# Sparse attention with a four-expert layer on one core: both phase-1 experts loaded early, probabilities normed before the split, q and k turned by DMA

## The chip, the cores and the metric

One core of one Trainium2 chip runs the kernel. The metric is device time in microseconds (us); a lower time is better. TensorE (PE) multiplies, VectorE (DVE), ScalarE (ACT) and GpSimd (POOL) do elementwise work, and SyncE (SP) only issues DMAs. Each engine runs its own instructions in the order in which the program lists them.

## The reference

```python
def _attn_ref(q, k, v, tau):                 # q, k, v: (4, 8, 576, 64) float32
    scores = (1 / sqrt(64)) * q @ k.transpose(0, 1, 3, 2)
    thresh = max(scores, -1) - tau           # keep what is within tau of the row's largest
    scores = where(scores >= thresh, scores, -1e9)
    attn = exp(scores - max(scores, -1))
    attn = attn / (sum(attn, -1) + 1e-9)
    return attn @ v
# x: (2304, 512), the 4 * 576 tokens with their 8 heads side by side
def _moe_ref(x, domain_probs, w1, w2):       # w1: (4, 512, 1024), w2: (4, 1024, 512)
    p = domain_probs / (sum(domain_probs, -1) + 1e-9)
    return sum over e of p[:, e:e+1] * (maximum(x @ w1[e], 0) @ w2[e])
```

Every token goes through all four experts.

## The kernel before

**Numbers.** Where float32 accuracy is wanted at float16 speed, a value is scaled by a power of two and split into a high and a low float16 half, `hi = f16(s*a)` and `lo = f16(s*a - hi)`, and a product is three matmuls: hi·hi, hi·lo, lo·hi. ACT writes the high half, DVE or POOL the low one. Weights, V, q and k of batches 1 to 3, and the probabilities of these batches go this way. Batch 0 is done in plain float32.

**Attention.** The work is cut into 80 items: 4 batches, 4 pairs of heads, and 5 blocks of query rows (`j` = 0 to 3 with 128 rows for each head of the pair, `j` = 4 with the last 64). Item 20 is the first of batch 1. In an item PE makes the scores in the one PSUM tile S (`emit_qk`), DVE copies them to SBUF as SS and takes the row's extreme (`cm`, L931), POOL adds tau to it (tile sm, L946), ACT takes the exponential into E (L954), and DVE sets to zero what is below the threshold and sums the rows (L963, both inputs in SBUF). The probabilities then have to be turned for the product with V. In batch 0 PE turns E through PSUM (tile ET) and ACT copies it to PT. From batch 1 on E is split (ACT L1069, DVE L1073) and a DMA transpose brings both halves to PT (`spread`, `turn`). `group` multiplies with V (tile av), and norms last: reciprocals of the row sums are spread over partitions by small matmuls (tile rp, L1140 and L1148) and multiplied in. The result is split into X, the input of the experts.

q and k come to SBUF as raw; `t_prep` turns them on PE through the tile S (10 float32 transposes a pair of heads, L601 to L606), and from batch 1 on ACT and DVE split them out of PSUM into T.

**Experts.** `unit` takes a block of tokens through one expert: G1 (tile mm from X and W, L1284), ReLU and split into h on ACT and POOL (L1296, L1304, L1313), G2 (L1328), and the accumulation. Experts 0 and 1 are phase 1 and run between the items; their partial sums go to DRAM. Experts 2 and 3 are phase 2 and run when phase 1 is done, since the 16 weight tiles W hold two experts. `ready` hands a block to `unit` when all four pairs of heads are done for its rows. `passes` says which `j` make a block: in batch 0 (0), (1), (2, 3, 4), else (0, 1), (2, 3, 4). The last blocks of all, 256 and 128 tokens, can run only after the last item.

**Order.** The class `Plan` lists operations with a cost and a priority each (item number for attention, 1000 and more for the experts), and writes them out engine by engine in the order of its own schedule. Pools limit it: 3 tiles raw, 3 tiles ss (SS and the split E), 2 tiles PT.

## Time and profile before

| | before |
|---|---|
| median of 3 runs | 1057.08 us (1055.54 to 1059.47) |
| the profiled execution's own time | 1056.98 us |
| its span, first to last instruction | 1055.2 us |
| PE busy | 1011.8 us, 96% of the span |
| DVE, ACT, POOL busy | 568.9, 571.8, 238.8 us |
| G1 and G2 on PE (L1284, L1328), busy | 376.4 and 395.4 us |

The span is shorter than the time by what lies around the first and last instruction, 1.8 us. Busy time of PE counts overlapping matmuls once. A share of busy time is a mean over stages: attention with the experts between it, the rest of phase 1, and phase 2.

### The profile page before, as it was taken

How to read it: one execution, taken by the hardware profiler on the slowest of the kernel's cores; microseconds unless marked ns; L12 is line 12 of the kernel's file. 1: busy time of each engine (PE TensorE's matmuls, PEld its weight loads, DVE VectorE, ACT ScalarE, POOL GpSimd, SP SyncE). 2: the span in 40 equal slices, each digit the busy share in tenths (PEclk: the TensorE clock that was granted, in tenths of full speed). 3: DMA queues.
4: the chain of work that ended last, by engine and by line, in shares of the span. 5: the costliest groups of instructions: out<-in, count | busy, mean ns of one | idle time of the engine just before them, and what ended most of it. 6: DMA issues, size and time to landing. Idle time of an engine off the chain costs nothing.

```text
span 1055.2 us, 20513 instructions
## 1 busy us (share of the span) xinstructions
PE 1011.8 (96%) x7946; PEld 665.4 (63%) x7946; DVE 568.9 (54%) x1338; ACT 571.8 (54%) x1183; POOL 238.8 (23%) x399
## 2 busy tenths in 40 slices
PE   6679969999999999999999999998999999999997
PEld 4466746666666567665656676665766676677665
DVE  3786767988779887888874005563221222122222
ACT  4777767766676668765664355543432343234322
POOL 1113325433344335333332232100000000000000
PEclk9889978999999999999999999999999999999999
DMA  6900325656558667555665103420201101011000
GB/s 172 248 12 18 93 82 137 125 91 142 103 107 190 91 121 117 112 103 110 123 113 108 40 2 123 147 71 30 91 10 51 40 21 61 21 41 40 1 31 21
DMA packets 211970, 88.67 MB, mean 84 GB/s; under 512 B 178336, under 2 KB 198816, under 8 KB 211872
## 3 DMA queue, kind: packets, MB, share of 16 engines
q1 hardware_dynamic: 211872, 87.36, 36.4%
q8 instruction: 62, 1.02, 0.4%
q14 instruction: 36, 0.29, 0.1%
HBM read 40.93 MB, written 14.16 MB: 52 GB/s over the span
## 4 chain that ended last, share of the span: by engine, by line
PE 83%; DMA 5%; DVE 4%; SPq 3%; ACT 2%; issue 2%; POOL 1%; DVEq 0%; ACTq 0%; POOLq 0%
PE mm L1284 34%; PE mm L1328 33%; PE av L1174 4%; PE S L865 4%; SPq L380 3%; DMA PT<-E 3%; DMA wraw<-in_moe_w_dram 2%; PE S L876 1%; DVE E L963 1%; PE av L1183 1%; PE ET L983 1%; DVE SS L931 1%; PE S L601 1%; PE rp L1140 1%; PE S L870 1%
## 5 line engine op out<-in xcount | busy, mean ns | idle before, releaser
L1328 PE MATMUL mm<-W,h 128*128 128x512 f16 x1728 | 395.4, 379 | 0.0
L1284 PE MATMUL mm<-X,W 128*128 128x256 f16 (+1 forms) x3360 | 376.4, 270 | 3.0 <-ACT hr L1296 3.0
L1284 PEld LDWEIGHTS <-W 128*128 128x128 f16 x3744 | 343.2, 98 | 56.3 <-issue 3.2
L1296 ACT ACTIVATE hr<-mm,wc 128x256 f32<-128x256 f32 (+1 forms) x312 | 141.6, 456 | 283.0 <-PE mm L1284 279.0
L1328 PEld LDWEIGHTS <-h 128*128 128x128 f16 x1728 | 165.2, 98 | 175.5 <-issue 0.4
L1313 POOL TENSOR_TENSOR h<-hr,h 128x256 f16<-128x256 f32 (+1 forms) x168 | 115.9, 696 | 143.8 <-ACT h L1304 119.1
L963 DVE SCALAR_TENSOR_TENSOR E<-SS,sm,E 128x576 f32<-128x576 f32 x144 | 123.0, 865 | 17.1 <-ACT E L954 10.6
L1353 DVE SCALAR_TENSOR_TENSOR acc<-mm,psc,acc 128x512 f32<-128x512 f32 x54 | 38.9, 748 | 169.7 <-PE mm L1328 169.4
L1313 DVE TENSOR_TENSOR h<-hr,h 128x256 f16<-128x256 f32 x144 | 60.9, 425 | 125.5 <-ACT h L1304 125.3
L946 POOL TENSOR_SCALAR sm<-sm,tau_p 128x1 f32<-128x1 f32 x144 | 77.4, 538 | 215.8 <-DVE SS L931 160.0
L1304 ACT ACTIVATE h<-hr 128x256 f16<-128x256 f32 (+1 forms) x312 | 122.4, 397 | 6.4
L954 ACT ACTIVATE E<-SS,sm 128x576 f32<-128x576 f32 x144 | 108.4, 767 | 15.8 <-DVE SS L931 15.7
L1268 POOL TENSOR_SCALAR psc<-pnv,wpm 128x2 f32<-128x2 f32 (+1 forms) x39 | 18.3, 474 | 348.3 <-DVE acc L1353 268.1
L931 DVE TENSOR_SCALAR_CACHE_REDUCE SS<-S,qc 128x576 f32<-128x576 f32 x108 | 85.7, 813 | 18.6 <-PE S L876 8.5
L1069 ACT ACTIVATE E<-E 128x1152 f16<-128x1152 f32 (+1 forms) x72 | 65.4, 924 | 44.9 <-DVE E L963 23.7
L1073 DVE SCALAR_TENSOR_TENSOR E<-E,E 128x1152 f16<-128x1152 f32 (+1 forms) x72 | 76.6, 1078 | 11.8 <-ACT E L1069 11.8
L1174 PE MATMUL av<-PT,V 128*64 128x320 f16 (+3 forms) x768 | 62.5, 311 | 2.1 <-DMA PT<-E 2.1
L865 PE MATMUL S<-T 64*128 64x512 f16 (+1 forms) x352 | 59.9, 442 | 1.6 <-DVE SS L931 0.9
L809 DVE SCALAR_TENSOR_TENSOR W<-wraw,wsc,W 128x1024 f16<-128x1024 f32 x28 | 35.4, 1285 | 37.7 <-ACT W L784 37.6
L784 ACT ACTIVATE W<-wraw,wsc 128x1024 f16<-128x1024 f32 x32 | 35.3, 1143 | 24.7 <-DVE wsc L454 24.3
L931 DVE TENSOR_SCALAR_CACHE_REDUCE SS<-S,qs 128x576 f32<-128x576 f32 x36 | 28.7, 812 | 22.9 <-PE S L876 15.1
L1174 PEld LDWEIGHTS <-V 128*64 128x64 f16 x576 | 31.3, 109 | 10.9 <-issue 6.9
(114 smaller groups left out, 689.8 us busy)
## 6 DMA issues: line engine op xcount, KB each, us to landing
wraw<-in_moe_w_dram SPq DMA_DIRECT2D x64, 256.0 KB, 3.9
part<-acc SPq DMA_DIRECT2D x18, 256.0 KB, 2.2
X<-x_dram SPq DMA_DIRECT2D x9, 512.0 KB, 3.6
acc<-part SPq DMA_DIRECT2D x18, 256.0 KB, 2.8
raw<-in_q_dram SPq DMA_DIRECT2D x32, 128.0 KB, 3.0
raw<-in_k_dram SPq DMA_DIRECT2D x32, 128.0 KB, 3.2
out_dram<-acc SPq DMA_DIRECT2D x16, 256.0 KB, 2.3
x_dram<-X SPq DMA_DIRECT2D x7, 512.0 KB, 3.0
```

The costliest lines, as they stand in the source:

```text
L865: nc.tensor.matmul(ps[:, 1024 * h:1024 * h + SM], t[r, a, 128 * j:128 * j + 128], t[r, c, 704:1216], start=(y == 0), stop=(y == last),)
L931: nc.vector.tensor_scalar(out=pl.t(*ssu)[:, S * h:S * h + S], in0=pl.t(*su)[:, 960 * h:960 * h + S], scalar1=qc[:, g, 2:3] if g >= NP * T3 ...
L946: lambda h=h: nc.gpsimd.tensor_scalar(out=pl.t(*mu)[:, 2 + h:3 + h], in0=pl.t(*mu)[:, h:h + 1], scalar1=tau_p, scalar2=1.0, op0=ALU.add, o ...
L954: lambda h=h: nc.scalar.activation(out=pl.t(*eu)[:, S * h:S * h + S], in_=pl.t(*ssu)[:, S * h:S * h + S], func=ACTF.Exp, scale=-1.0, bias= ...
L963: lambda h=h, col=col: nc.vector.scalar_tensor_tensor(out=pl.t(*eu)[:, S * h:S * h + S], in0=pl.t(*ssu)[:, S * h:S * h + S], scalar=pl.t(* ...
L1073: nc.vector.scalar_tensor_tensor(out=o, in0=e, scalar=2.0**12, in1=h, op0=ALU.mult, op1=ALU.subtract)
L1174: nc.tensor.matmul(av[64 * h:64 * h + 64, 0:n], va(slice(0, 128), vp, 4 * h + c), t[:, 5 * h + c, tp, 0:n], start=(c == 0 and y == 0), sto ...
L1284: nc.tensor.matmul(ps[:, 0:n], w[:, wp, 0, c * 128:(c + 1) * 128], x[:, c, xp, c0:c0 + n], start=(i == 0), stop=(i == len(seq) - 1),)
L1296: lambda mu=mu, hru=hru, f=f: nc.scalar.activation(out=pl.t(*hru)[:, 0:n], in_=pl.t(*mu)[:, 0:n], func=ACTF.Relu, scale=wc[:, e, f:f + 1],),
L1304: lambda hu=hu, hru=hru: nc.scalar.activation(out=pl.t(*hu)[:, 0, 0:n], in_=pl.t(*hru)[:, 0:n], func=ACTF.Copy),
L1313: lambda hu=hu, hru=hru, ap=ap: ap.tensor_tensor(out=pl.t(*hu)[:, 1, 0:n], in0=pl.t(*hru)[:, 0:n], in1=pl.t(*hu)[:, 0, 0:n], op=ALU.subtra ...
L1328: nc.tensor.matmul(ps, h[:, hp, 128 * i:128 * i + 128], w[:, wp, 1, :], start=(f == f0 and hp == 0 and wp == 0), stop=(f == f1 - 1 and hp ...
```

## The change: what it does

- **Four items only in float32.** The first block of batch 0 (4 items) keeps the way through PE and ET. The other 16 items of batch 0 go the way of split and DMA transpose. q and k of batch 0 stay float32.
- **Normed, then split.** Each item takes its reciprocals on DVE (`rec`, L994 and L997). In the 20 items of batch 0 POOL multiplies E by them (L1008), and in 16 of them POOL also makes the low half (L1124, L1130). From batch 1 on the reciprocal is the scale of the split itself, one piece for each head. The small matmuls rp and the multiplication behind av are gone. High and low halves are turned by a DMA each.
- **q, k by DMA.** For batches 1 to 3 `t_turn` splits raw (and the tail tile tl) in SBUF into R, and one DMA transpose makes T of it.
- **Both experts' weights at once.** Expert 1's weights are loaded right behind those of expert 0, six of its eight blocks into the two tiles of PT. Their high halves are made on POOL (`hi_gp`, L788), their low halves on DVE.
- **Blocks of 128 tokens.** Batches 0 and 1 are cut into passes (0), (1), (2), (3, 4), and each block goes through both experts at once.
- V of batch 0 is split too; V has 9 blocks instead of 10. Some costs of the plan are other numbers.

```diff
-    passes = {0: ((0,), (1,), (2, 3, 4))}
+    passes = {0: ((0,), (1,), (2,), (3, 4)), 1: ((0,), (1,), (2,), (3, 4))}
...
+    def t_turn(g, prio):
...
+        for c, n, u in ((0, 1024, ru), (8, 256, tl)):
+            act(
+                n / 1.1 + 200,
+                lambda c=c: nc.scalar.activation(
+                    out=views(c, 0)[0], in_=views(c, 0)[1], func=ACTF.Copy, scale=qc[:, g, 0:1]
+                ),
...
+            dve(
+                n / 0.84 + 80,
+                lambda c=c: nc.vector.scalar_tensor_tensor(
+                    out=views(c, 1)[0], in0=views(c, 1)[1], scalar=qc[:, g, 0:1],
+                    in1=views(c, 0)[0], op0=ALU.mult, op1=ALU.subtract,
+                ),
...
+        pl.op(
+            "SP", 475,
+            lambda: nc.sync.dma_start(
+                out=pl.t(*T).rearrange("p c x n -> p (c x) n"),
+                in_=pl.t(*R).rearrange("p c x k -> p (c x k)"), transpose=True,
+            ),
...
+            if hi_gp(f):
+                gp(
+                    1120,
+                    lambda x=x, W=W, f=f: nc.gpsimd.tensor_scalar(
+                        out=pl.t(*W)[:, 0], in0=x(), scalar1=wsc[:, e, f:f + 1], scalar2=1.0,
+                        op0=ALU.mult, op1=ALU.mult,
+                    ),
...
+        turned = pooled(i)
+        if one or turned:
+            for h in heads:
+                gp(
+                    650,
+                    lambda h=h: nc.gpsimd.tensor_scalar(
+                        out=pl.t(*eu)[:, S * h:S * h + S], in0=pl.t(*eu)[:, S * h:S * h + S],
+                        scalar1=pl.t(*ru)[:, h:h + 1], scalar2=1.0, op0=ALU.mult, op1=ALU.mult,
+                    ),
...
+    def pooled(i):
+        return NF32 <= i < 20
...
+                    nc.gpsimd.tensor_tensor(
+                        out=pl.t(*fu)[:, 1, 0:9].rearrange("p c k -> p (c k)"), in0=pl.t(*eu),
+                        in1=pl.t(*fu)[:, 0, 0:9].rearrange("p c k -> p (c k)"), op=ALU.subtract,
+                    )
...
-        if name == ("m", 0, 0):
+        if name == ("m", 0, 0) and 0:
             return
...
+        for f in range(NF):
+            w_load(1, f, "wrawP", -2 + f)
+        P1 = lambda f: 4.5 + 0.3 * f
+        for f in range(0, NF, 4):
+            at(3, w_prep, 1, f, 4, "wrawP", P1, True, lambda f: f in (), lambda f: f < 8)
```

Two places show how the instructions move. The first is POOL in the middle of batch 0. Before (sm is the threshold of an item, h the low half behind the ReLU, pnv the scaled expert probabilities, wraw and W the weights of expert 1):

```order
L946 TENSOR_SCALAR sm<-sm,tau_p 128x1
L1313 TENSOR_TENSOR h<-hr,h 128x128 x3
L946 TENSOR_SCALAR sm<-sm,tau_p 128x1 x3
L704 TENSOR_SCALAR pnv<-pn,v_c 128x16
L709 TENSOR_SCALAR pnv<-pn,v_c 64x4
L946 TENSOR_SCALAR sm<-sm,tau_p 128x1 x3
L792 TENSOR_SCALAR wraw<-wraw,wsc 128x1024
```

The same engine in the middle of batch 0 after the change (E at L1008 is the norming, E at L1124 the low half of an item's probabilities):

```order
L1008 TENSOR_SCALAR E<-E,ri 128x576
L963 TENSOR_SCALAR sm<-sm,tau_p 128x1
L1338 TENSOR_TENSOR h<-hr,h 128x128
L963 TENSOR_SCALAR sm<-sm,tau_p 128x1
L1124 TENSOR_TENSOR E_1625<-E,E_1625 128x1152
L1338 TENSOR_TENSOR h<-hr,h 128x128 x2
L1008 TENSOR_SCALAR E<-E,ri 128x576
L1338 TENSOR_TENSOR h<-hr,h 128x128
```

Where POOL took a threshold, a few h and now and then a weight, each item now brings two normings and a low half of 1152 columns besides, and the threshold of the next item stands among them.

The second place is SP near the end of batch 0. Before, it loads raw of batch 1 and weights of expert 1 (vr is V, x_dram the stored input of phase 2):

```order
L380 DMA raw<-in_q_dram 128x4x64 x2
L380 DMA raw<-in_k_dram 128x4x64 x2
L380 DMA wraw<-in_moe_w_dram 128x4x128
L380 DMA wraw<-in_moe_w_dram 128x512
L380 DMA wraw<-in_moe_w_dram 128x4x128
L380 DMA wraw<-in_moe_w_dram 128x512
L380 DMA raw<-in_q_dram 128x4x64 x2
```

After the change the weights are gone from there, and transposes of batch 0's probabilities (PT) and of q and k (T from R) stand between the loads:

```order
L1087 DMA_TRANSPOSE PT<-E_1959 128x5x64 x4
L655 DMA_TRANSPOSE T_2040<-R_1985 128x20x128
L376 DMA raw<-in_q_dram 128x4x64
L1087 DMA_TRANSPOSE PT<-E_2097 128x9x128
L376 DMA raw<-in_q_dram 128x4x64
L376 DMA raw<-in_k_dram 128x4x64
L1087 DMA_TRANSPOSE PT<-E_2097 128x9x128
L376 DMA part_135<-acc 128x512
```

On PE, ahead of item 20's scores, the program before lists 192 matmuls G1 of 128 columns, 72 of 256 and 48 of G2; the changed one lists 576 of 128 columns and 126 of G2. Behind the scores of item 20 the program before has 8 turns of q and k and 252 small matmuls rp; the changed one has neither.

## Rows read from the trace of the kernel before

**Rows 1.** Busy time of each engine by stretch; then clock, DMA share and GB/s.
```profile
0.00:62.00 62.00, 43.08 (x241) 26.84 (x242) 35.14 (x112) 36.53 (x66) 7.80 (x29) 0.86 0.69 179
62.00:170.00 108.00, 95.59 (x784) 65.03 (x784) 77.45 (x213) 82.20 (x186) 39.89 (x66) 0.92 0.22 57
170.00:572.00 402.00, 398.93 (x3592) 254.88 (x3591) 324.62 (x760) 274.56 (x541) 159.91 (x245) 1.00 0.62 120
572.00:674.00 102.00, 102.00 (x791) 69.17 (x790) 25.69 (x43) 46.14 (x103) 25.46 (x44) 1.00 0.23 75
674.00:1055.20 381.20, 372.25 (x2545) 249.45 (x2542) 106.00 (x213) 132.36 (x288) 5.72 (x16) 0.99 0.13 41
```

**Rows 2.** PE in order of time: the scores of item 20 (start, duration, what).
```profile
170.13 0.82 PE L865 MATMUL S<-T 64*128 64x512 f16 x6
```

**Rows 3.** The chain that ended last, from 560 us: start, duration, what.
```profile
571.85 10.47 PE mm L1328 x48
582.32 10.48 PE mm L1284 x96
592.80 10.36 PE mm L1328 x48
```

**Rows 4.** PE in order of time: turning q and k, and what starts behind it.
```profile
393.32 1.04 PE L601 MATMUL S<-ident,raw 128*128 128x128 f32 x8
394.66 1.50 PE L1284 MATMUL mm<-XT,W 128*128 128x128 f16 x24
```

**Rows 5.** PE in order of time: the matmuls rp, and what starts behind them.
```profile
260.29 0.41 PE L1140 MATMUL rp<-ident,r 128*64 128x128 f16 x8
...
260.81 0.82 PE L865 MATMUL S<-T 64*128 64x512 f16 x6
```

**Rows 6.** PE in order of time: G1 of 128 columns, and what starts behind it.
```profile
109.39 0.83 PE L1284 MATMUL mm<-X,W 128*128 128x128 f16 x12
110.06 0.61 PE L983 MATMUL ET<-ident,E 128*128 128x128 f32 x4
```

**Rows 7.** PE in order of time: products with V, and what starts behind them.
```profile
232.20 1.50 PE L1174 MATMUL av<-PT,V 128*64 128x256 f16 x24
...
233.99 0.81 PE L870 MATMUL S<-T 64*64 64x512 f16 x6
...
248.02 1.82 PE L1174 MATMUL av<-PT,V 128*64 128x320 f16 x24
...
250.20 0.83 PE L870 MATMUL S<-T 64*64 64x512 f16 x6
```

**Rows 8.** DVE in order of time: two maskings of E behind each other.
```profile
18.88 0.81 DVE L963 SCALAR_TENSOR_TENSOR E<-SS,sm,E 128x576 f32<-128x576 f32 x1
...
19.62 0.82 DVE L963 SCALAR_TENSOR_TENSOR E<-SS,sm,E 128x576 f32<-128x576 f32 x1
```

**Rows 9.** POOL in order of time, around 126 us.
```profile
123.75 1.12 POOL L792 TENSOR_SCALAR wraw<-wraw,wsc 128x1024 f32<-128x1024 f32 x1 [0.73 <-ACT W L784]
...
126.19 2.13 POOL L801 TENSOR_TENSOR W<-wraw,W 128x1024 f16<-128x1024 f32 x1
```

**Rows 10.** DVE in order of time, around 126 us.
```profile
124.73 1.28 DVE L809 SCALAR_TENSOR_TENSOR W<-wraw,wsc,W 128x1024 f16<-128x1024 f32 x1 [1.15 <-ACT W L784]
126.78 2.15 DVE L963 SCALAR_TENSOR_TENSOR E<-SS,sm,E 128x576 f32<-128x576 f32 x1 [0.77 <-ACT E L954]
```

**Rows 11.** Lines one by one: count, shortest, median and longest (ns), first and last start.
```profile
L946 POOL TENSOR_SCALAR sm<-sm,tau_p x144: 260/268/1989, 17.1 to 558.3; 128x1 f32<-128x1 f32 x144
L1313 POOL TENSOR_TENSOR h<-hr,h x168: 422/671/1540, 72.4 to 663.0; 128x256 f16<-128x256 f32 x120, 128x128 f16<-128x128 f32 x48
L1045 SPq DMA_TRANSPOSE PT<-E x72: 1205/2688/6065, 183.3 to 566.4; - x72
```

**Rows 12.** DVE in order of time: item 20's first masking of E.
```profile
174.70 0.82 DVE L963 SCALAR_TENSOR_TENSOR E<-SS,sm,E 128x576 f32<-128x576 f32 x1 [1.56 <-POOL h L1313]
```

More of the change, by code (lines that the diff above doesn't have):

```diff
@@ L646, in v_prep @@
+    def v_prep(b, prio0, prio, prio1=None):
         st, V = ("st", ("v", b)), ("vr", b)
-        vu = [("V32", (b, pr)) if b < V32 else V for pr in range(NP)]
-        view = lambda pr: pl.t(*vu[pr]) if b < V32 else pl.t(*V)[:, pr]
         parts = []
@@ L723, in v_prep @@
             )
-        for pr in range(NP) if b >= V32 else ():
+        for pr in range(NP):
             u = ("V", (b, pr))
             act(
-                720,
+                770,
                 lambda pr=pr, u=u: nc.scalar.activation(
@@ L882, in emit_qk @@
             for h in range(2):
-                r = slice(64 * h, 64 * h + 64)
                 nc.tensor.matmul(
-                    ps[r, SM:S], t[r, a, SM:S], t[r, c, S + 64 * h:S + 64 * h + 64],
-                    start=(y == 0), stop=(y == last),
+                    ps[rows(h), SM:S], qm(h, a), ktt(h, c), start=(y == 0), stop=(y == last),
                 )
@@ L971, in item, with rec @@
         c0 = 128 * main.index(j) if j < 4 else 128 * nm
+        nh = len(heads)
+        if one:
+            pl.reserve(("SS", i + 1))
+        def rec():
+            r = pl.t(*ru)[:, 0:nh]
+            nc.vector.tensor_scalar(
+                out=r, in0=r, scalar1=1e-9, scalar2=2.0**-15, op0=ALU.add, op1=ALU.mult
+            )
+            nc.vector.reciprocal(out=r, in_=r)
+        dve(
+            340, rec, [("ri", i, h) for h in heads], [("ri", i)], use=[ru], prio=i + 0.2,
+        )
+        turned = pooled(i)
[6 more added lines that the diff above has]
+                        scalar1=pl.t(*ru)[:, h:h + 1], scalar2=1.0, op0=ALU.mult, op1=ALU.mult,
+                    ),
+                    [("E", i, h), ("ri", i)], [("E", i, h)], use=[eu, ru], prio=i + 0.2,
+                )
         if not one:
@@ new lines, in spread, with hi, lo @@
+        for h in heads if not turned else ():
+            def hi(h=h):
+                for o, e in parts(0, h):
+                    nc.scalar.activation(
+                        out=o, in_=e, func=ACTF.Copy, scale=pl.t(*ru)[:, h:h + 1]
+                    )
+            def lo(h=h):
+                for (o, e), (hh, _) in zip(parts(1, h), parts(0, h)):
+                    nc.vector.scalar_tensor_tensor(
+                        out=o, in0=e, scalar=pl.t(*ru)[:, h:h + 1], in1=hh, op0=ALU.mult,
+                        op1=ALU.subtract,
+                    )
+            act(
+                700 if j < 4 else 980, hi, [("E", i, h), ("ri", i)], [("eh", i, h)],
+                use=[eu, fu, ru], prio=i + 0.2,
+            )
+            dve(
+                680 if j < 4 else 820, lo, [("E", i, h), ("ri", i), ("eh", i, h)],
+                [("el", i, h)], use=[eu, fu, ru], prio=i + 0.2,
+            )
@@ new lines, in spread @@
+        for x in range(2):
+            keys = [("eh" if x == 0 else "el", i, h) for h in heads]
+            if j < 4:
+                turn(
+                    i,
+                    lambda x=x: pl.t(*fu)[:, x, 0:9].rearrange("p c k -> p (c k)"),
+                    lambda x=x: pl.t(*pu)[:, x, 0:9, c0:c0 + 128],
+                    72 * 16, keys, [("PT", i, x, 0)], [fu, pu],
+                )
+            for h in range(2 if j == 4 else 0):
+                turn(
+                    i,
+                    lambda x=x, h=h: pl.t(*fu)[64 * h:64 * h + 64, x, 0:5].rearrange(
+                        "p c k -> p (c k)"
+                    ),
+                    lambda x=x, h=h: pl.t(*pu)[:, x, 5 * h:5 * h + 5, c0:c0 + 64],
+                    20 * 16, keys, [("PT", i, x, h)], [fu, pu],
+                )
@@ L1188, in av_ @@
                     nc.tensor.matmul(
[L1189 to L1190 removed]
+                        av[64:128, k:n], va(slice(64, 128), vp, 8),
+                        ts(slice(64, 128), tp, 9, k, n), start=False, stop=end,
                     )
         pe(
[L1194 removed]
+            200 + n * 8.6 if one else 24 * max(45, 0.235 * n) + 6 * max(60, 0.34 * n), av_,
             ([("PT", i, x, 0) for i in its for x in ((0, 1, 2) if items[i][1] < 4 else (0, 1, 2, 3))]
[L1196 to L1198 removed]
+             if one else
+             [("PT", i, x, h) for i in its for x in range(2) for h in range(1 if items[i][1] < 4 else 2)])
+            + ([("v", b, pr), ("v", b, NP), ("v", b, NP + 1)] if one
                else [("vh", b, pr), ("vl", b, pr)]),
             [("av", gi)], use=[pu, au, V], prio=last + 1.1,
[L1201 to L1207 removed]
         )
```

438 lines of the change are left out of this document (174 added, 264 removed), and 4 rows, old and new, of the table pools.

## The prediction

> **What bounds the kernel now.** I read the busy time by stretch first [rows 1]. From 170 to 674 us PE is idle for 3.1 us of 504, at full clock (1.00, the 2.4 GHz level), while DVE is busy for 81% of 170 to 572 and POOL for 40%. Behind 674 us, in phase 2, PE is idle for 9 us of 381. So from 170 us on the time is the sum of what PE does. Before 170 us it is not: PE is busy for 43 of the first 62 us and for 96 of the next 108, at a mean clock of 0.86 and 0.92, and DVE, ACT and POOL are busy for 113, 119 and 48 of the 170 us. No engine is full there; items pass from one engine to the next, and each waits in turn. The reader should therefore cut the span at one instruction, the scores of item 20 at 170.1 us [rows 2]. Ahead of it a chain sets the pace, behind it PE's sum does. The chain that ended last agrees: from 572 us on it is G1 and G2 without a break [rows 3].
>
> The sum is made against the profiled execution: span 1055.2 us, time 1056.98 us, so 1.8 us lie around the span. The median of the runs shown is 1057.08 us, the same within 0.1 us.
>
> **Behind item 20: what PE no longer does there.** The span leaves 1055.2 - 170.1 = 885.1 us. Prices are distances from one start to the next, since durations of PE overlap.
>
> - *Experts done earlier.* A G1 of 256 columns costs 10.48/96 = 0.1092 us, a G2 10.36/48 = 0.2158 us [rows 3], a G1 of 128 columns 0.67/12 = 0.0558 us [rows 6]. Ahead of item 20 stood 192 x 0.0558 + 72 x 0.1092 + 48 x 0.2158 = 28.9 us of them; now stand 576 x 0.0558 + 126 x 0.2158 = 59.3 us, because each block of 128 tokens goes through both experts at once. 30.4 us more are done early. Cutting 672 G1 of 256 columns in two costs 672 x 0.0024 = 1.6 us. Net -28.8 us.
> - *q and k by DMA.* A turn on PE takes 1.34 us [rows 4]. Eight of twelve stood behind item 20: -10.7 us.
> - *No spreading of reciprocals.* Twelve matmuls rp take 0.52 us [rows 5]; 252 stood there: -10.9 us.
> - *Products with V.* A group of 256 columns takes 1.79 us, one of 320 takes 2.18 us [rows 7]. Before, twelve of each stand behind item 20, and one float32 group that I price like a 320 one: 49.8 us. Now there are eight of each, 31.8 us, and batch 1's smaller groups: twelve of 128 columns and six of 192. No row shows these. By columns alone they would cost 0.90 and 1.34 us, by their count of matmuls as much as 1.79 us each. I take 1.35 and 1.60, the middle: 57.6 us in all, +7.8 us (+0.9 at the low end, +14.2 at the high end).
>
> Sum: -42.6 us, so 842.5 us stay behind item 20 (836 to 849).
>
> Can DVE keep that pace? By the matmuls that stand behind the last product with V (96 G1 of 256 columns and 54 G2 fewer than before, 22 us) its 60 items get about 380 us instead of 402. DVE's work in them hardly changes: the split of E becomes two pieces, a small reciprocal per item comes, the multiplication behind av goes, and the low half of q and k is read from SBUF instead of PSUM. 325 us of 380 are 85%, so PE stays the bound; the cover is thinner than before.
>
> **Ahead of item 20.** PE loses the turns of E of 16 items and four turns of q and k, and gains 30 us of experts; 139 us of busy time become some 150 in a stretch longer than that. ACT trades copies out of PSUM for casts, and expert 1's bounds for the high halves that POOL now makes. DVE trades one thing for another likewise. I cost these at nothing; what hides them is the slack of some 50 us that each of these engines has there [rows 1]. The weights of both experts now stand at the head of SP's queue, behind q, k and V, and what they push back is batch 1's loads, which are needed only much later. Six blocks of expert 1 lie in the two tiles PT, so no item of the new kind can be turned before they are split; PE has the first block's G1 and G2 to do meanwhile.
>
> POOL is another matter. Up to item 20's first masking it now does 36 thresholds (0.268 us), 48 h of 128 columns (0.422 us) [rows 11], 16 high halves of weights (1.12 us), 12 low halves of 1152 columns (2.13 us for 1024, so 2.40), three shorter ones (1.33) and 36 normings of 576 columns [rows 9]. No row has a norming: one column costs 0.268, 1024 columns cost 1.12 us, and by columns it is 0.75. With some 25 small ones at 0.27 that is 9.6 + 20.3 + 17.9 + 28.8 + 4.0 + 27.0 + 6.8 = 114 us (97 to 128 by the bounds of the norming), against 48 us busy before.
>
> And POOL's time is not its own. POOL's instruction from 126.19 to 128.32 us [rows 9] stands over a masking of E on DVE that started at 126.78 and took 2.15 us [rows 10] instead of 0.82 [rows 8]: it ended 0.6 us behind POOL's end, so it waited. Both read SBUF, the masking through two inputs. The Trainium skill says this outright ("SBUF — State Buffer", section "SBUF: two separate sides"): a GpSimd instruction and a VectorE instruction with two SBUF inputs hold one shared port pair in turn, each for its whole length. Here the trace agrees, with 2.15 against 0.82 us; by the page's rule taken strictly the sum would be the one that I work out next, and without it POOL's 114 us would hide in the stretch.
>
> So I add what must alternate. On DVE these are 36 maskings (0.74 us from start to start [rows 8]), 16 low halves of weights (1.28 us [rows 10]), six of V and three of q and k (0.72 and 1.60 us, by their columns): 26.6 + 20.5 + 4.3 + 4.8 = 56 us. With POOL's 114 us that is 170 us. Counted from POOL's first threshold at 17.1 us [rows 11] item 20 would reach its first masking at 187 us. In the trace that is at 174.7 us [rows 12], 4.6 us behind its scores, so the scores stand at about 183 us instead of 170. The ends of instructions overlap a little, which makes it less; gaps make it more. At the low end nothing is lost (170 us), at the high end the norming costs 1.12 us (196 us). I take 183.
>
> **Sum.** 183 + 842.5 + 1.8 = 1027 us, 2.8% under the median. Something like 43 us are gained behind item 20 and 13 given back ahead of it.
>
> **Rivals.**
>
> - *POOL is hidden.* POOL fits between DVE's instructions, as it does from 170 to 572 us, where it is busy for 160 of 402 us and the maskings are rarely late. Item 20 comes at 170 us or before: 170 + 842.5 + 1.8 = 1014 us or less. Against it: POOL alone would have to be busy for 114 of 153 us, close to twice the share.
> - *The DMA queue is late in batches 1 to 3.* Nine transposes of q and k stand behind item 20; with 20 blocks instead of 18 each holds the queue for about 2.69 x 20/18 = 3.0 us [rows 11], 27 us in a stretch where the DMA engines are busy for 62% already. If PE waited for all of it: 1027 + 27 = 1054 us. Against it: raw comes many items ahead.
> - *The thresholds stand behind the low halves: no gain, or slower.* One threshold of item i+1 is queued on POOL behind a low half of item i, and DVE's masking, all later DVE work and the next scores queue behind that. If each of 36 maskings were late by 2.15 - 0.82 = 1.33 us, as the one at 126.78 was, item 20 would come at 170 + 48 = 218 us, and the time be 218 + 842.5 + 1.8 = 1062 us. It turns to slower than before once item 20 comes later than 213 us.
>
> **How the numbers follow.** I give the forecast (item 20 at 176 to 200 us, 1020 to 1044) 0.52, the hidden POOL 0.25, the late queue 0.10, and the queued thresholds 0.13. The range of 8 in 10 goes from 1000, where the first case would also start its experts earlier, to 1056, which holds most of the late queue. Half a percent, 5.3 us, is about what a measurement of this kernel can tell from no change. Faster than 1051.8 are the forecast, the hidden POOL and part of the late queue: 0.85. Within half a percent lie the rest of that case and half of the last: 0.08. Slower: 0.07.
>
> **What would show it.** In the profile of the changed kernel: the first float16 scores near 183 us, and PE's stretch from there to the end near 842 us with few idle microseconds; POOL busy for about 115 us before item 20; normings near 0.75 us and low halves near 2.4 us where nothing blocks them, and maskings of E far over 0.82 us where POOL's instruction covers them; products with V of 128 columns near 1.35 us. The prediction is wrong if PE waits much for transposes of PT or T in batches 1 to 3, if item 20 comes after 208 us or before 170, or if the last product with V is much later than 565 us.

## The result, and the profile after

The changed kernel takes 1062.9 us (median of 5 runs, 1060.98 to 1067.0) against 1057.1: a ratio of 1.0058 [1.0033, 1.0083]. It is slightly slower; the prediction was 1027 us with a range to 1056. The profiled execution took 1061.64 us, 1.7 us more than its span of 1059.9.

Busy time by stretch, with the columns of [rows 1]:

```profile
0.00:62.00 62.00, 41.22 (x246) 25.70 (x246) 41.24 (x99) 41.28 (x74) 32.34 (x46) 0.85 0.82 219
62.00:170.00 108.00, 88.49 (x956) 59.85 (x957) 82.50 (x178) 62.27 (x160) 97.23 (x119) 0.88 0.55 101
170.00:572.00 402.00, 364.03 (x3833) 239.69 (x3832) 322.71 (x793) 282.76 (x637) 174.93 (x296) 0.97 0.74 135
572.00:674.00 102.00, 102.00 (x847) 68.14 (x846) 46.33 (x95) 55.02 (x119) 32.65 (x52) 1.00 0.41 104
674.00:1059.90 385.90, 380.33 (x2616) 255.62 (x2614) 103.42 (x206) 136.05 (x296) 4.62 (x16) 1.00 0.12 39
```

PE is busy for 976.1 us where it was 1011.8 before: the work went, as the change meant. But PE's idle time went from 43.4 to 83.8 us. The new idle time lies in the third row, 38.0 us of 402 where [rows 1] has 3.1, beside a DMA share of 0.74 instead of 0.62 and a clock of 0.97 instead of 1.00. The two instructions at which the prediction cuts the span, PE in order of time:

```profile
183.21 0.82 PE L889 MATMUL S<-T 64*128 64x512 f16 x6
...
601.78 1.82 PE L1203 MATMUL av<-PT,V 128*64 128x320 f16 x24
```

Item 20's scores stand where the prediction put them (183), the last product with V 37 us later than it said (565), which it had named as a sign of being wrong. Cut there, in the same columns:

```profile
183.21:250.00 66.79, 48.94 (x578) 32.50 (x578) 48.43 (x112) 42.53 (x103) 26.48 (x46) 0.85 0.80 142
250.00:601.78 351.78, 333.42 (x3372) 218.60 (x3369) 286.30 (x713) 252.22 (x557) 148.19 (x250) 0.99 0.71 131
601.78:1059.90 458.12, 452.55 (x3214) 304.84 (x3213) 129.49 (x249) 170.65 (x373) 27.23 (x52) 1.00 0.15 49
```

From item 20 to the last product with V, PE is idle for 17.9 + 18.4 = 36.2 us of 418.6 (these differences are of rounded rows). The waits of all engines from 170 to 602 us that bear on it (waiting engine and line, what it waited for: us, times, longest):

```profile
ACT E L1144 <- DMA PT<-E: 16.6, 9, 3.4
PE av L1203 <- DMA PT<-E: 15.3, 13, 4.2
...
PE S L889 <- DVE SS L948: 13.6, 7, 8.0
...
ACT R L640 <- DMA PT<-E: 10.7, 8, 2.5
...
DVE SS L948 <- DMA T<-R: 5.2, 4, 2.2
```

PE waits for transposes directly and for DVE's copies of scores; ACT and DVE wait, before they write E16, R or SS, for a transpose to land. The longest such wait, all engines in order of time (start, duration; in brackets the idle time before it and what ended it):

```profile
195.65 0.80 DVE L948 TENSOR_SCALAR_CACHE_REDUCE SS<-S,qc 128x576 f32<-128x576 f32 x1
...
196.64 1.15 ACT L640 ACTIVATE R<-raw,qc 128x1024 f16<-128x1024 f32 x1 [2.17 <-DMA PT<-E]
197.24 3.80 SPq L1087 DMA_TRANSPOSE PT<-E  x3
...
199.03 0.48 DVE L647 SCALAR_TENSOR_TENSOR R<-tl,qc,R 128x256 f16<-128x256 f32 x1
199.42 0.81 DVE L948 TENSOR_SCALAR_CACHE_REDUCE SS<-S,qc 128x576 f32<-128x576 f32 x1
...
200.29 1.46 PE L889 MATMUL S<-T 64*128 64x512 f16 x6 [8.02 <-DVE SS L948]
...
201.14 3.11 SPq L655 DMA_TRANSPOSE T<-R  x1
...
204.30 4.11 SPq L1087 DMA_TRANSPOSE PT<-E  x3
206.30 0.82 DVE L948 TENSOR_SCALAR_CACHE_REDUCE SS<-S,qc 128x576 f32<-128x576 f32 x1 [1.93 <-DMA T<-R]
206.80 1.92 PE L1203 MATMUL av<-PT,V 128*64 128x192 f16 x21 [4.16 <-DMA PT<-E]
```

Read from the top: R is one of the three tiles ss, so ACT can write it only when a PT transpose has landed and given one back. DVE makes R's low half, and its second copy of the scores stands behind that; PE, which has one tile S for scores, waits 8.02 us for it. Of these, 3.0 us lie between the end of the first copy (196.45) and the start of the second (199.42), where R stands; the others go to the two copies and to DVE's work ahead of the first. R keeps its tile until T<-R has landed: the copy at 206.30 waits for that. Meanwhile the turn of E at 204.30 stands on SP's queue behind T<-R, and PE's product with V waits 4.16 us for it.

**Three numbers of every run.** PE's idle time ahead of item 20's scores, the same up to the last product with V, and the clock between these two, each worked out from the windows cut at these instructions. The plan makes the order anew for every edit, so a run also moves things that its edit does not name; the controls show by how much. The runs were made in five groups (e1 to e4, e5 to e8, e9 to e12, e13 to e15, e16 and e17); the kernel before, run again in each, took 1056.1 to 1058.5 us at the median. A difference of 2 or 3 us between runs of different groups therefore shows nothing.

| kernel | time, us | item 20 at | idle ahead | idle to last V | clock |
|---|---|---|---|---|---|
| before | 1057.1 | 170.1 | 31.3 | 3.1 | 1.00 |
| changed | 1062.9 | 183.2 | 42.0 | 36.2 | 0.97 |
| e1: q, k on PE | 1044.1 | 192.1 | 41.8 | 10.0 | 0.99 |
| e2: batch 1's passes as before | 1069.1 | 186.6 | 46.3 | 40.1 | 0.95 |
| e3: four tiles ss | 1056.3 | 186.9 | 46.0 | 24.4 | 0.97 |
| e4: its control | 1070.7 | 192.0 | 47.8 | 33.2 | 0.95 |
| e5: before + q, k by DMA | 1056.8 | 153.7 | 27.4 | 15.7 | 0.97 |
| e6: its control | 1057.9 | 167.6 | 31.7 | 2.7 | 1.00 |
| e7: e1, three raw | 1052.8 | 199.4 | 44.7 | 11.9 | 0.99 |
| e8: e7 + 12 idle transposes | 1072.8 | 200.8 | 47.4 | 20.9 | 0.96 |
| e9: changed, T from ACT | 1088.4 | 197.0 | 48.5 | 47.2 | 0.95 |
| e10: e1, no POOL in items | 1038.7 | 188.9 | 40.5 | 9.9 | 0.99 |
| e11: e1, half of it on POOL | 1043.8 | 192.1 | 43.0 | 11.3 | 0.99 |
| e12: e1, eight float32 items | 1044.7 | 191.2 | 40.2 | 9.5 | 1.00 |
| e13: e10, no low halves of expert 1 | 1025.7 | 178.6 | 31.1 | 7.5 | 1.00 |
| e14: e10, some of them on POOL | 1041.9 | 190.8 | 39.4 | 10.9 | 0.99 |
| e15: changed, no POOL in items | 1056.6 | 181.9 | 44.5 | 31.9 | 0.97 |
| e16: e10, high halves on ACT | 1036.2 | 186.3 | 36.6 | 9.5 | 0.99 |
| e17: e10, expert 1's on ACT | 1039.7 | 189.6 | 36.8 | 10.1 | 0.99 |

### The profile page after: what moved, and what is told of

It is laid out like the page before. It is cut to its first block, busy times and chain, and to the rows that moved or that the text cites. A ratio compares the mean times of both kernels' runs of the same rounds, so it can differ in the third digit from the quotient of the medians.

```text
span 1059.9 us, 22238 instructions
## 1 busy us (share of the span) xinstructions
PE 976.1 (92%) x8492; PEld 649.0 (61%) x8492; DVE 596.2 (56%) x1369; ACT 577.4 (54%) x1283; POOL 341.8 (32%) x526
## 3 DMA queue, kind: packets, MB, share of 16 engines
q8 instruction: 66, 1.08, 0.4%
## 4 chain that ended last, share of the span: by engine, by line
PE 67%; DMA 11%; DVE 10%; issue 4%; POOL 3%; SPq 3%; ACT 2%; DVEq 0%; ACTq 0%; POOLq 0%
PE mm L1309 29%; PE mm L1353 29%; DMA PT<-E 5%; PE S L889 3%; DMA T<-R 3%; PE av L1203 3%; DVE E L979 2%; DVE SS L948 2%; SPq L376 2%; DVE W L822 2%; DVE E L1150 1%; DMA wrawP<-in_moe_w_dram 1%; DMA wraw<-in_moe_w_dram 1%; POOL h L1338 1%; SPq L1087 1%
## 5 line engine op out<-in xcount | busy, mean ns | idle before, releaser
L1309 PEld LDWEIGHTS <-W 128*128 128x128 f16 x4416 | 366.6, 99 | 67.6 <-issue 5.9
L1309 PE MATMUL mm<-X,W 128*128 128x256 f16 (+1 forms) x4032 | 391.7, 255 | 5.0 <-DVE X L1248 2.0
L1321 ACT ACTIVATE hr<-mm,wc 128x256 f32<-128x256 f32 (+1 forms) x368 | 155.2, 424 | 303.6 <-PE mm L1309 291.6
L1338 POOL TENSOR_TENSOR h<-hr,h 128x128 f16<-128x128 f32 (+1 forms) x224 | 148.4, 670 | 137.7 <-ACT h L1329 85.5
L979 DVE SCALAR_TENSOR_TENSOR E<-SS,sm,E 128x576 f32<-128x576 f32 x144 | 127.2, 894 | 29.6 <-POOL sm L963 14.4
L971 ACT ACTIVATE E<-SS,sm 128x576 f32<-128x576 f32 x144 | 109.2, 767 | 28.4 <-DVE SS L948 13.9
L1150 DVE SCALAR_TENSOR_TENSOR E<-E,ri,E 128x576 f16<-128x576 f32 (+1 forms) x120 | 91.5, 788 | 18.3 <-ACT E L1144 17.8
L1144 ACT ACTIVATE E<-E,ri 128x576 f16<-128x576 f32 (+1 forms) x120 | 83.9, 723 | 29.0 <-DMA PT<-E 16.6
L889 PE MATMUL S<-T 64*128 64x512 f16 (+3 forms) x440 | 79.4, 464 | 15.9 <-DVE SS L948 14.1
L1203 PE MATMUL av<-PT,V 128*64 128x128 f16 (+3 forms) x1056 | 59.8, 257 | 22.9 <-DMA PT<-E 22.6
L1203 PEld LDWEIGHTS <-V 128*64 128x64 f16 x1056 | 45.1, 113 | 37.9 <-issue 24.3
L822 DVE SCALAR_TENSOR_TENSOR W<-wraw,wsc,W 128x1024 f16<-128x1024 f32 x26 | 36.8, 1445 | 34.1 <-ACT W L797 33.8
L889 PEld LDWEIGHTS <-T 64*128 64x128 f16 (+1 forms) x360 | 14.6, 98 | 35.0 <-issue 24.6
```

The lines of the kernel that those rows point to most:

```text
L889: nc.tensor.matmul(ps[:, 1024 * h:1024 * h + SM] if j < 4 else ps[rows(h), 0:SM], qm(h, a), km(h, c), start=(y == 0), stop=(y == last),)
L971: lambda h=h: nc.scalar.activation(out=pl.t(*eu)[:, S * h:S * h + S], in_=pl.t(*ssu)[:, S * h:S * h + S], func=ACTF.Exp, scale=-1.0, bias= ...
L979: lambda h=h: nc.vector.scalar_tensor_tensor(out=pl.t(*eu)[:, S * h:S * h + S], in0=pl.t(*ssu)[:, S * h:S * h + S], scalar=pl.t(*mu)[:, 2 ...
L1144: nc.scalar.activation(out=o, in_=e, func=ACTF.Copy, scale=pl.t(*ru)[:, h:h + 1])
L1150: nc.vector.scalar_tensor_tensor(out=o, in0=e, scalar=pl.t(*ru)[:, h:h + 1], in1=hh, op0=ALU.mult, op1=ALU.subtract,)
L1203: nc.tensor.matmul(av[64 * h:64 * h + 64, 0:n], va(slice(0, 128), vp, 4 * h + c), ts(slice(0, 128), tp, 5 * h + c, 0, n), start=(c == 0 an ...
```

## Experiments on the idle time behind item 20

**e1, q and k back on PE.** `t_prep`, the layout of T and `emit_qk` as before; R and its transposes are gone.

```diff
...
-                at(int(c0 + .5), t_turn, b * NP + pr, c0 + 0.5)
+                at(t0 - 7 + 2 * pr, t_prep, b * NP + pr, t0 - 7 + 2 * pr)
```

> The changed kernel, but q and k of batches 1 to 3 are transposed by TensorE into the score tile again, as before; R16 and its transposes T<-R are gone. Theory Q (the q,k halves sit in one of the three score-sized tiles and their transposes hold the one DMA queue, so scores, splits and turns of batches 1 to 3 come late, and TensorE idles 45 us between item 20's scores and the last product with V): TensorE's work grows by 10.7 us, the idle time falls by 30 to 40 us, time 1033 to 1045. Rival P (batch 1's groups of one item with two PT tiles make TensorE wait): idle time falls by less than 10 us, time 1064 to 1074.

1044.08 us, 0.9869 [0.9852, 0.9886] of before: 18.8 us less than the changed kernel, though PE does the turns again (985.0 us busy in the whole kernel instead of 976.1). The stretch from 170 to 572 us:

```profile
170.00:572.00 402.00, 392.02 (x4110) 258.80 (x4109) 337.29 (x841) 296.63 (x663) 177.38 (x305) 0.99 0.66 121
```

PE is idle there for 10.0 us instead of 38.0, and its wait for PT (av on DMA PT<-E) is 3.1 us up to 602 us instead of 15.3. Up to the last product with V the idle time falls by 26.2 us (36.2 to 10.0), a little less than the 30 to 40 that theory Q gave; its time came, and rival P falls. Against the saving of 10.7 us that the sum counts, q and k by DMA cost 18.8 + 10.7 = 29.5 us. Behind item 20 alone the cost is larger, since item 20 comes 8.9 us later in e1. The sum of e1's windows from item 20 to the end:

```profile
sum 850.40, PE 834.71 PEld 559.23 DVE 455.08 ACT 459.62 POOL 190.47; mean PE 278.24 PEld 186.41 DVE 151.69 ACT 153.21 POOL 63.49
```

850.4 us, where the changed kernel takes 876.7.

**e2, batch 1 in the passes of before.**

```diff
-    passes = {0: ((0,), (1,), (2,), (3, 4)), 1: ((0,), (1,), (2,), (3, 4))}
+    passes = {0: ((0,), (1,), (2,), (3, 4))}
```

> The changed kernel, but batch 1 goes through its queries in passes (0,1) and (2,3,4), as before, so a PT tile serves two or three items and batch 1 has 8 products with V in place of 16. Theory P: the 26 us of idle time up to 300 us and the low clock there go, time 1030 to 1042. Rival Q: only the cheaper products with V show (about 4 us), time 1055 to 1063, and TensorE still idles 35 us or more between item 20's scores and the last product with V.

1069.09 us, 1.0108 [1.008, 1.0136]; idle time to the last product with V rises to 40.1 us. Theory P falls. Rival Q's idle time is there (35 us or more), its time (1055 to 1063) is not: the small groups of batch 1 are worth 6.2 us here, and why stays open.

**e3 and e4, a fourth tile ss, and the control.** Both have the smaller load and h pools; only e3 has the tile.

```diff
-("raw", 4) ... ("ss", 3) ... ("h", 8)
+("raw", 3) ... ("ss", 4) ... ("h", 7)     (e3)
+("raw", 3) ... ("ss", 3) ... ("h", 7)     (e4)
```

> The changed kernel with four score-sized tiles (ss) in place of three; the room comes from one load tile (raw 4 to 3, as before) and one h tile (8 to 7). Theory Q: R16 no longer takes a tile from scores and E16, so the waits of ACT for DMA PT<-E and of PE for DVE SS fall to a third, time 1035 to 1048. If the DMA queue itself is late, or by rival P: 1058 to 1066.

> Control of the run before: the changed kernel with raw 4 to 3 and h 8 to 7 alone, three score-sized tiles. Every theory: 1060 to 1068, as the changed kernel; more than that would be the price of the smaller load pool, to be taken off the run with four tiles.

1056.28 us (0.9979 [0.996, 0.9997]) and 1070.66 us (1.0122 [1.0091, 1.0152]). The control is 7.8 us above the changed kernel, more than expected: the smaller pools have a price. Against it the fourth tile gives 14.4 us, and idle time to the last product falls from 33.2 to 24.4. 1056 us lies above what theory Q gave for a tile that explains all: the tile that R takes is a large part of the cost, but 24.4 us of idle time are left, where e1 has 10.0.

**e5 and e6, the edit alone on the kernel before.** R, `t_turn` and the new layout of T put into the kernel before, h 8 to 7 for room; e6 has h 7 alone.

```diff
-                at(t0 - 7 + 2 * pr, t_prep, b * NP + pr, t0 - 7 + 2 * pr)
+                at(t0 - 7 + 2 * pr, t_turn, b * NP + pr, t0 - 7 + 2 * pr)
```

> The kernel before with one part of the change alone: q and k of batches 1 to 3 split before they are turned (R16 in one of the three score-sized tiles) and transposed by DMA; h tiles 8 to 7 to make room. By the prediction's term TensorE loses 10.7 us of work and the time falls to 1046 to 1050. Theory Q (the shared tile and the queue cost 30 us of idle time): the time rises to 1066 to 1082, with 20 us or more of new idle time between 170 and 570 us. Rival R (the transposes of q and k only hurt where batch 0's items use the queue too): 1046 to 1058.

> Control of the run above: the kernel before with h tiles 8 to 7 alone. Every theory: 1055 to 1063; what it is above the kernel before is taken off the run above.

1056.78 us (0.9976 [0.9959, 0.9992]) and 1057.94 us (1.0004 [0.9987, 1.002]). The edit is worth 1.2 us there, not 10.7: 9.5 us are lost, and idle time to the last product goes from 2.7 to 15.7 us. Theory Q's size was wrong for this kernel; rival R has it. In a kernel whose batch 0 sends no turns of its own the same edit loses a third of the 29.5 us; other parts differ as well, so the run agrees with R's reason and does not single it out. The small loss also hides two larger changes: by the spans, item 20 comes 13.9 us earlier than in e6, and what stands behind it takes 15.2 us longer (901.9 against 886.7).

**e7 and e8, transposes that nobody waits for.** To e1 with three raw tiles (the control) 12 transposes of T into a tile without readers are added; no tile ss is taken.

```diff
...
+        if two:
+            pl.op(
+                "SP", 475,
+                lambda: nc.sync.dma_start(
+                    out=dum_t, in_=pl.t(*T).rearrange("p x n -> p (x n)"), transpose=True
+                ),
+                [("T", g, c, x) for c in (0, 1024) for x in range(2)], [("dum", g)],
+                use=[T], prio=prio, xfer=-152 * 16,
+            )
```

> Control of the next run: the changed kernel with q and k on TensorE in batches 1 to 3 (1044 us) with load tiles raw 4 to 3. Every theory: 1043 to 1054.

> The control above with 12 more DMA transposes of 19 chunks on the one queue, one behind each T of batches 1 to 3, into a tile that nobody reads; no score-sized tile is taken and no work waits for what they write. Theory Q1 (the queue's time alone costs most of what the score-sized tile does not explain, 10 us or more): 10 to 20 us above the control, with waits of TensorE for DMA PT<-E of 10 us or more. Theory Q2 (the queue has room; it is the wait for T itself and the order of the queue's in-order waits): within 4 us of the control.

1052.81 us (0.9946 [0.9921, 0.9971]) and 1072.82 us (1.012 [1.0085, 1.0155]). The control is 8.7 us above e1: the change also has a fourth tile raw, which its list does not name, and with q and k on PE this tile is worth that much. Twelve transposes cost 20 us though no instruction needs what they write. The stretch from item 20 to the last product, first of the control, then with them:

```profile
199.41:589.73 390.32, 378.42 (x3960) 250.81 (x3961) 323.79 (x811) 287.87 (x646) 161.62 (x285) 0.99 0.67 122
```

```profile
200.79:609.75 408.96, 388.11 (x3956) 256.60 (x3953) 323.45 (x811) 290.40 (x646) 165.07 (x285) 0.96 0.71 130
```

Of the 18.6 us between them 9.0 are idle time (20.9 against 11.9) and 9.7 are the same work at a lower clock (388.1 against 378.4 us for as many matmuls, 0.96 against 0.99). PE's waits for PT from 170 to 610 us, first of the control:

```profile
PE av L1176 <- DMA PT<-E: 5.1, 9, 1.0
```

```profile
PE av L1186 <- DMA PT<-E: 13.3, 18, 1.6
```

Theory Q1 holds: the queue's time alone delays the turns of E that PE needs. It also keeps the tiles ss longer: DVE's copies of scores wait 12.3 us for PT<-E there, 4.7 in the control. So tile and queue are not two separate costs.

**e9, T from ACT's queue.**

```diff
-            "SP", 475,
-            lambda: nc.sync.dma_start(
+            "ACT", 475,
+            lambda: nc.scalar.dma_start(
                 out=pl.t(*T).rearrange("p c x n -> p (c x) n"),
```

> The changed kernel with the 12 transposes T<-R issued from ACT in place of SP: another queue, the same bytes, the same 16 DMA engines, R16 still in a score-sized tile; ACT now stands at each of them until its issue is over. If it is the order on the one queue that costs (T<-R waits for R's low half, PT turns and loads stand behind it): 1040 to 1052. If it is the time on the DMA engines, or the tile that R16 holds: 1058 to 1068; above that, ACT's own issuing of them costs (3 to 4 us each, 12 of them: up to 40 us more).

1088.37 us, 1.0297 [1.0273, 1.0322]. The 12 issues on ACT's queue, in ns (shortest, median, longest), and how long a T takes to land, shortest, median and longest in us:

```profile
L658 ACTq DMA_TRANSPOSE T<-R x12: 3079/3769/5020, 158.4 to 510.7; - x12
...
DMA to landing us min/median/max: 4.9/7.8/10.0
```

ACT spends 12 x 3.77 = 45 us on them, and a T lands in 7.8 us, where it takes 5.5 in the changed kernel. Whether two queues turn faster than one is not shown, since in this run they never turn at once:

```profile
177.02 4.80 ACTq L658 DMA_TRANSPOSE T<-R  x1
...
186.20 7.93 SPq L1090 DMA_TRANSPOSE PT<-E  x6
```

In all twelve cases SP ends the issue of its last turn of E at least 1.2 us before T starts, and the next one starts 5.0 to 10.2 us behind T's start, where it is 3.2 to 5.9 us in the changed kernel. So this run adds two prices, ACT's issuing and turns kept apart, and it does not test another queue at work beside the first. How much of the cost on one queue is its order and how much the time on the DMA engines stays open.

## Experiments on the time ahead of item 20

**e10, e11 and e15, batch 0 without GpSimd.** `pooled` says which items POOL norms and splits; elsewhere ACT and DVE scale in the split, as in batches 1 to 3.

```diff
     def pooled(i):
-        return NF32 <= i < 20
+        return False                          (e10 on e1, e15 on the changed kernel)
+        return NF32 <= i < 20 and i % 2 == 0  (e11 on e1)
```

> The changed kernel with q and k on TensorE in batches 1 to 3 (1044 us), and batch 0's other 16 items scaled in the split on ACT and DVE, as in batches 1 to 3, with nothing of it on GpSimd. By the prediction's model of batch 0 (GpSimd's 114 us and DVE's two-input work take turns, and item 20 comes at 183 to 192 us for it): GpSimd's 130 us falls to about 70, DVE gains 16 times 1.6 us = 25 us, item 20 comes at 165 to 180 us and the time is 1025 to 1038. Rival (DVE and ACT take over as the bound of batch 0, or its DMA does): 1040 to 1055.

> As the run above, but every second of these 16 items stays on GpSimd. By the prediction's model: item 20 at 165 to 182 us, time 1026 to 1040, at most a few us from the run above; by the rival as 1044, within 6.

> The changed kernel with the 16 items of batch 0 scaled in the split on ACT and VectorE, nothing of it on GpSimd; q and k still by DMA. If only the 5 us show that the same edit gave with q and k on TensorE: 1055 to 1060. If late low halves on GpSimd hold score-sized tiles that R16 needs: 1042 to 1053.

1038.66 us (0.9826 [0.9805, 0.9846]), 1043.83 (0.9871 [0.9847, 0.9894]) and 1056.62 (0.9976 [0.9957, 0.9995]). POOL's time from 62 us to item 20 falls from 116.3 (e1) to 63.5 us (e10), and item 20 comes at 188.9 instead of 192.1, not at 165 to 180; e10's time lies just above the model's range and below the rival's, and e11 came as the rival had it. The idle time ahead of item 20 hardly moves (41.8, 40.5). So the sum of POOL's and DVE's time does not set item 20's time; DVE's own load, which grows in the exchange, is not ruled out by these runs. That the two hold each other up is seen in the maskings of E between 62 us and item 20 (count | busy us, mean ns | idle before), of e1:

```profile
L952 DVE SCALAR_TENSOR_TENSOR E<-SS,sm,E 128x576 f32<-128x576 f32 x25 | 26.5, 1069 | 11.3 <-POOL sm L936 7.1 <-ACT E L944 2.7 <-POOL E L1103 1.6
```

and of e10:

```profile
L952 DVE SCALAR_TENSOR_TENSOR E<-SS,sm,E 128x576 f32<-128x576 f32 x24 | 20.5, 870 | 1.2 <-ACT E L944 1.2
```

With POOL out of the items, 6 us of the maskings and 10 us of the waits in front of them are gone, and DVE's own low halves (22 of 0.91 us, 19.8 us) fill the place. e15 gives 6.3 us on the changed kernel by the medians, e10 on e1 5.4 (8.7 and 4.5 by the ratios to the kernel before of each group). Idle time to the last product is still 31.9 us in e15: late low halves on POOL are at most a small part of what holds the tiles that R needs.

**e12, eight float32 items.**

```diff
-    NF32 = NP
+    NF32 = 2 * NP
```

> The changed kernel with q and k on TensorE in batches 1 to 3 (1044 us), and eight items in place of four in float32: four items fewer to split on GpSimd (4 times 2.4 us) and to turn by DMA (8 turns), four more with float32 transposes and products on TensorE (about 4 us each). If GpSimd holds batch 0: 1036 to 1044. If TensorE's own work counts there: 1046 to 1056.

1044.66 us (0.9878 [0.9852, 0.9904]), as e1, and between what the two theories expected: inconclusive.

**Where the idle time lies.** Before item 20 the idle time is not spread. The stretch from 40 to 100 us, of before, of the changed kernel and of e10, in the columns of [rows 1]:

```profile
40.00:100.00 60.00, 49.10 (x430) 34.19 (x429) 47.23 (x146) 45.48 (x100) 10.85 (x29) 0.91 0.25 60
```

```profile
40.00:100.00 60.00, 37.62 (x309) 24.31 (x307) 55.81 (x90) 33.68 (x77) 53.99 (x48) 0.73 0.50 122
```

```profile
40.00:100.00 60.00, 35.09 (x326) 24.11 (x327) 56.54 (x106) 34.47 (x75) 40.88 (x37) 0.79 0.49 120
```

PE's idle time there is 10.9, 22.4 and 24.9 us, and DVE is nearly full in the last two: it splits weights of both experts in one go, and items stand behind.

**e13, expert 1's low halves left out.** They are set to zero by DVE, so that part of the products is left out.

```diff
+            if e == 1:
+                dve(
+                    400, lambda W=W: nc.vector.memset(pl.t(*W)[:, 1], 0.0),
+                    rr + [("wh", e, f)], [("wl", e, f)], use=[u, W], prio=prio(f),
+                )
+                continue
```

> The run without GpSimd in batch 0 (q and k on TensorE, 1038.7 us), with the low halves of expert 1's weights set to zero by VectorE in place of being computed: this leaves out part of the computation, so its output differs slightly. If VectorE's 16 more low halves at 40 to 100 us hold batch 0 back (theory W): TensorE's idle time from 40 to 100 us falls from 25 us by 10 us or more, time 1020 to 1030. If not (the loads, or items' own chain): 1034 to 1039.

1025.67 us (0.9698 [0.9672, 0.9724]), 13.0 less than e10; item 20 comes at 178.6, and the idle time ahead of it is 31.1 us, as before the change. The same stretch:

```profile
40.00:100.00 60.00, 43.95 (x403) 29.15 (x403) 53.99 (x130) 41.07 (x98) 41.73 (x50) 0.77 0.52 125
```

PE is idle for 16.0 us in place of 24.9, 8.9 less, where theory W gave 10 or more; the time is in its range, and the other theory falls. Theory W holds in the main. Expert 1 has eight blocks, so eight low halves are left out here and not 16. Up to 192 us DVE spends 27.7 us on the weights' low halves in e10, and 18.8 with the eight fillings of zeros in e13; these 8.9 us are near the 10.3 by which item 20 comes earlier.

**e14, every second low half of expert 1 on GpSimd.**

```diff
-            at(3, w_prep, 1, f, 4, "wrawP", P1, True, lambda f: f in (), lambda f: f < 8)
+            at(3, w_prep, 1, f, 4, "wrawP", P1, True, lambda f: f % 2 == 1, lambda f: f < 8 and f % 2 == 0)
```

> The same run with every second low half of expert 1's weights on GpSimd (about 4 us each there, in two instructions), the arithmetic whole. Theory W, if GpSimd's work runs beside VectorE's: 1028 to 1035. If GpSimd and VectorE take turns, nothing is won: 1037 to 1046.

1041.91 us (0.9846 [0.9828, 0.9865]), not apart from e10 (0.9826 [0.9805, 0.9846]): nothing is won, as the second theory gave. PE's idle time from 40 to 100 us falls all the same, from 24.9 to 21.0 us, and item 20 comes no earlier (190.8 against 188.9), so the reason is not shown to be the two engines' turns.

**e16 and e17, high halves of weights on ACT.** `hi_gp` of both experts (e16) or of expert 1 (e17):

```diff
-            at(1, w_prep, 0, f, 4, "wraw0", EP, True, GP0, lambda f: f < 8)
+            at(1, w_prep, 0, f, 4, "wraw0", EP, True, GP0, lambda f: False)     (e16)
...
-            at(3, w_prep, 1, f, 4, "wrawP", P1, True, lambda f: f in (), lambda f: f < 8)
+            at(3, w_prep, 1, f, 4, "wrawP", P1, True, lambda f: f in (), lambda f: False)     (e16, e17)
```

> The run without GpSimd in batch 0 (q and k on TensorE, 1038.7 us), with the high halves of both experts' weights on ACT in place of 16 on GpSimd. If the two engines hold each other up at 40 to 100 us: VectorE's low halves take 1.28 us in place of 1.79 and 1.73, TensorE's idle time there falls from 25 us by 5 us or more, time 1028 to 1035. If ACT (34 of 60 us busy there, plus 16 times 1.14 us) takes over as what holds: 1036 to 1046.

> The same with the high halves of expert 1's weights alone on ACT (8 times 1.14 us), expert 0's still on GpSimd. If the engines hold each other up: 1031 to 1037, expert 1's low halves at 1.28 us. If not: 1037 to 1041.

1036.19 us (0.981 [0.9774, 0.9846]) and 1039.67 (0.9846 [0.9817, 0.9876]). The weights' instructions from 40 to 100 us (count | busy us, mean ns | idle before), first e10:

```profile
L798 DVE SCALAR_TENSOR_TENSOR W<-wraw,wsc,W 128x1024 f16<-128x1024 f32 x10 | 17.4, 1791 | 0.6 <-POOL W L764 0.6
...
L764 POOL TENSOR_SCALAR W<-wraw,wsc 128x1024 f16<-128x1024 f32 x10 | 17.9, 1802 | 1.6 <-DVE wpow L453 1.6
```

then e16:

```profile
L798 DVE SCALAR_TENSOR_TENSOR W<-wraw,wsc,W 128x1024 f16<-128x1024 f32 x10 | 12.2, 1278 | 0.8 <-ACT W L773 0.8
L773 ACT ACTIVATE W<-wraw,wsc 128x1024 f16<-128x1024 f32 x10 | 10.7, 1135 | 0.0
```

The same low half takes 1.79 us beside GpSimd and 1.28 beside ACT. Idle time from 40 to 100 us falls by 3.5 us (24.9 to 21.4, from 38.63 us busy), less than the 5 expected; ACT is now busy for 53.9 of these 60 us. The time is 2.5 us under e10's, which two groups of runs do not tell apart. e17 gains nothing, though expert 1's low halves take 1.28 us in it too. e16 has the lowest time of a version that computes everything, 1.9% faster than before.

## Why the prediction was wrong

The sum was 183 + 842.5 + 1.8. Measured in the profiled execution: 183.2 + 876.7 + 1.7.

- **The step that failed: "q and k by DMA", priced at -10.7 us, with "few idle microseconds" behind item 20.** The sum took the turns off PE and set nothing against it. R lives in one of three tiles ss from ACT's split until T has landed, and T<-R stands on the queue that carries every turn of E. Idle time behind item 20 is 41.8 us where the sum kept the 12.0 of before; these 29.8 us are most of the miss of 34.2. With q and k back on PE (e1) 850.4 us stand behind item 20, near the 853.2 that the sum gives without this term (842.5 + 10.7). So by these two runs the term measured +26.3 us (876.7 - 850.4) instead of -10.7, and the rest of the sum nearly holds. Even PE's busy time behind item 20 does not show the saving: 834.9 us, and 834.7 in e1 with the turns in it, at a mean clock of 0.98 and 0.99 and with plans that also differ ahead of item 20. e4 to e3 show the tile (14.4 us), e7 to e8 the queue (20 us); together they exceed the 29.5 us of e1, so they overlap, and plans made anew blur both.
- **The rival that came nearest.** "The DMA queue is late in batches 1 to 3" named the place and a price, 27 us, and got a chance of 0.10. Even with PE waiting for all of it, its 1054 us lie under the 1062.9 measured: it had the queue and not the tile. The reason against it, "raw comes many items ahead", looked at the start of the chain only: R cannot be written before a tile is free and T's place in the queue comes. Its 3.0 us for each transpose was near: 3.53 us is the median here.
- **The lower clock** was no term at all. From 183 to 250 us it is 0.85, with 48.9 us of busy time: up to some 7 us, by an estimate from that row (48.9 x 0.15).
- **Ahead of item 20 the number was right by luck.** The working, GpSimd's 114 us and DVE's 56 in turn, gives 183, and 183.2 was measured. But with GpSimd's time from 62 us to item 20 about halved (116.3 to 63.5 us in e10, 107.5 to 58.3 in e15) item 20 moves by 3.2 and 1.3 us, not by tens. The prediction cited the Trainium skill ("SBUF — State Buffer", section "SBUF: two separate sides") for the shared port. The maskings bear it out (1.07 us on average in e1, 0.87 in e10); that the sum of both sets the pace of the whole stretch did not follow. What the runs show in its place are DVE's low halves of the weights at 40 to 100 us: e13, without those of expert 1, brings item 20 10.3 us earlier than e10. The prediction had the 16 of them in its sum, at 20.5 us, but of DVE's own load it said that it "trades one thing for another" and set the cost at nothing, under a slack of 50 us that is a mean over 170 us. In this stretch DVE was busy for 47 of 60 us already, with 8 of these low halves; now there are 16, most of them slowed beside GpSimd, 28.0 us in place of 10.0 (before, then the changed kernel, count | busy us, mean ns | idle before):

```profile
L809 DVE SCALAR_TENSOR_TENSOR W<-wraw,wsc,W 128x1024 f16<-128x1024 f32 x8 | 10.0, 1278 | 1.2 <-ACT W L784 1.2
```

```profile
L822 DVE SCALAR_TENSOR_TENSOR W<-wraw,wsc,W 128x1024 f16<-128x1024 f32 x10 | 16.6, 1703 | 0.2 <-POOL W L788 0.2
L822 DVE SCALAR_TENSOR_TENSOR W<-wrawP,wsc,W 128x1024 f16<-128x1024 f32 x6 | 11.4, 1922 | 2.2 <-POOL W L788 2.2
```

- **GpSimd's work** ahead of item 20 was 140 us instead of 115. The forms were priced rightly where nothing blocks them: normings 0.744 us at the median (0.75 predicted), low halves 2.372 (2.40). Blocked ones are longer: the normings' mean is 0.89.
- **Products with V** came cheaper. A group of 128 columns takes 256.01 - 254.93 = 1.08 us (1.35 taken), one of 192 columns 331.31 - 329.82 = 1.49 (1.60), so the term is 12 x 1.08 + 6 x 1.49 + 31.8 - 49.8 = +3.9 us instead of +7.8:

```profile
254.93 0.86 PE L1203 MATMUL av<-PT,V 128*64 128x128 f16 x24
255.72 0.35 PE L1212 MATMUL av<-PT,V 64*64 64x128 f16 x6
256.01 0.82 PE L889 MATMUL S<-T 64*128 64x512 f16 x6
...
329.82 1.18 PE L1203 MATMUL av<-PT,V 128*64 128x192 f16 x24
...
331.31 0.82 PE L1353 MATMUL mm<-W,h 128*128 128x512 f16 x3
```

- **Experts earlier and no rp**: not tested alone. PE's busy time behind item 20 is 834.7 us in e1, where the sum without its term for q and k implies 841.2 (853.2 less 12.0 idle); 3.9 of the difference are the products with V, so no large term of PE's work was wrong.

What stays open: how the cost divides between the tile and the queue, and how the queue's 20 us divide between its order and the DMA engines' time.

## What to carry to other kernels

When work moves from an engine to a DMA, price the tile that its source and target hold until the transfer has landed, and the queue that it shares with transfers on the critical path; here the engine time saved (10.7 us by the prediction's price) was the smaller part. A slack is to be read from the stretch in which the new work will stand, not from a mean over a longer one. A forecast that hits a time by a sum of two engines' work is not shown until one of the two is taken away.
